# A grouped-query attention kernel whose start is rearranged: more filler matmuls, K of group 1 transposed later, exp of chunk 1 in two parts, one more share for VectorE

## Chip, cores, metric

One core of a Trainium2 chip. The time is what the device takes for one execution, in microseconds (us). Before: 522.71 us, median of 3 runs (522.05 to 522.73). Times inside a trace are us from the start of the span.

## The reference

```python
B, Hq, Hkv, Sq, Sk, D = 16, 32, 8, 288, 512, 128        # bf16
k = jnp.repeat(k, Hq // Hkv, axis=1); v = jnp.repeat(v, Hq // Hkv, axis=1)
scores = jnp.einsum("bhqd,bhkd->bhqk", q, k) * D ** -0.5
p = softmax(scores, axis=-1)
return jnp.einsum("bhqk,bhkd->bhqd", p, v)
```

There are 128 groups (batch and KV head), each with 1152 query rows against 512 keys.

## The kernel before

A group's transposed scores are cut into three chunks of 1536 columns; there are NS = 384 chunks. For chunk n, TensorE makes the scores S(n) (three matmuls of 512 columns, or two of 512 and four of 128), ScalarE takes the exp, and two chunks later TensorE multiplies by V (the PV batch, twelve matmuls of 129 columns, the last column giving the row sums). VectorE divides. In every sixth chunk VectorE computes the exp of the last 120 columns itself (a polynomial): the "share"; TensorE makes those scores in a small matmul of its own.

K of groups 0 and 1 is transposed on TensorE (`op_kt`, four 128x128 transposes into PSUM) and copied to SBUF by VectorE (`op_kc`); later groups come transposed from the DMA. The parts that matter:

```python
FIRST = 2; FIRST_SHARED = 6; LAG = 2; EVERY = 6; W = 120; WARM = 5
...
def shared(n):
    return FIRST_SHARED <= n < NS - NC and (n - FIRST_SHARED) % EVERY == 0
...
# op_exp: chunks 0, 1 and the last are taken in three parts of 512 columns
if n < FIRST or n == NS - 1:
    parts = [(x, x + BANK) for x in range(0, CH, BANK)]
...
@block.tensor
def _(eng):
    op_warm(WARM, BANK, ps_o[:, 1])          # 5 matmuls of ones, 512 columns
    op_warm(1, P, ps_o[:, 1])
    op_kt(0, range(1), 0)                    # K of group 0
    op_kt(0, range(1, NJ), 1)
    op_warm(1, P, ps_s[:, 1])                # one more, 128 columns
    for n in range(NS):
        op_s(n)
        if shared(n):
            op_sy(n)
        if n == 2:
            op_kt(1, range(NJ), 1)           # K of group 1; chunk 3 is its first user
        if n >= LAG:
            op_pv(n - LAG)
...
@block.scalar
def _(eng):
    op_kd(eng, 0)                            # load of K of group 0
    eng.activation(dum[:], ...)
    for (s, n) in need(eng, [("s_k0", 2)]):  # both copies of K of group 0 are made
        eng.wait_ge(s, n)
    op_kd(eng, 1)                            # load of K of group 1
    for n in range(NS):
        op_exp(n)
```

The first queries come by a transposing DMA on another queue.

## Time and profile before

| | before |
|---|---|
| span of the profiled run | 520.0 us |
| first score matmul, first exp | 4.41, 5.05 |
| six chunks in the middle | 7.98 |
| last exp starts, last VectorE instruction (the flag, the kernel's own check of its sums) starts | 515.82, 518.40 |

How to read it: the middle repeats every six chunks, so a change in the 7.98 counts 63 times and a change at either end once. The page's "chain that ended last" is followed back from the last instruction, at each step to what released it; it and the first microseconds are shown in the prediction. View: DMA issues of the kernel before, in the window 4.25 to 4.5 (what is loaded, KB, us from issue to landing):

```profile
kd_sb<-in_k_dram ACTq DMA_DIRECT2D x1, 128.0 KB, 3.0
```

K of group 1 was issued at 4.27 and landed at 7.26.

### The profile page before, as it was taken

The page shows a single profiled execution, that of the slowest core. Times are in us where ns is not written, and L with a number is a line of the kernel's source. Part 1 is how long each engine was busy: PE and PEld are TensorE (multiplying, and loading weights), DVE is VectorE, ACT ScalarE, POOL GpSimd, SP SyncE. Part 2 cuts the span into 40 slices and gives each one's busy share as a digit, 9 for nine tenths or more (in the row PEclk, how much of TensorE's full clock was granted, in tenths as well). Part 3 has the DMA queues.
Part 4 walks back from the last instruction along what each step waited for, and adds up shares of the span by engine and source line. Part 5 has one row for each costly group of instructions (what it writes and reads, how often), then busy time and mean ns, then how long its engine had stood idle before and what let it go on. Part 6 is the DMA issues. An engine that isn't in the chain of part 4 may idle for free.

```text
span 520.0 us, 15243 instructions
## 1 busy us (share of the span) xinstructions
PE 510.3 (98%) x6118; PEld 394.6 (76%) x6224; DVE 369.6 (71%) x1315; ACT 513.3 (99%) x393; POOL 79.8 (15%) x135
## 2 busy tenths in 40 slices
PE   8999999999999999999999999999999999999997
PEld 5777777777777777777777777777777777777776
DVE  2767767777777677676776776767767767677776
ACT  7999999999999999999999999999999999999997
POOL 2111111111111111111111111111111111111110
PEclk9999999999999999999999999999999999999999
DMA  9999999999999998999999989999998989998212
GB/s 186 237 218 230 267 194 248 225 213 210 219 233 256 208 245 201 235 248 240 215 241 209 209 225 220 241 185 209 229 240 232 227 194 201 192 234 198 86 69 93
DMA packets 253078, 110.06 MB, mean 212 GB/s; under 512 B 219728, under 2 KB 236752, under 8 KB 253008
## 3 DMA queue, kind: packets, MB, share of 16 engines
q1 hardware_dynamic: 252720, 108.82, 97.7%
q8 instruction: 49, 0.80, 0.7%
q10 hardware_dynamic: 288, 0.26, 0.2%
q14 instruction: 21, 0.17, 0.2%
HBM read 17.04 MB, written 37.75 MB: 105 GB/s over the span
## 4 chain that ended last, share of the span: by engine, by line
ACT 98%; DMA 1%; issue 1%; DVE 0%; PE 0%
ACT pt_sb L516 97%; DMA qt_sb<-in_q_dram 1%; ACT pt_sb L511 1%; PE ps_s L439 0%; DVE o_sb L585 0%; DVE o_sb L595 0%; PE ps_s L479 0%; DVE rl_sb L575 0%; PE ps_o L669 0%; DVE bad_sb L621 0%; DVE flag_i L734 0%; DVE bad_sb L618 0%
## 5 line engine op out<-in xcount | busy, mean ns | idle before, releaser
L516 ACT ACTIVATE pt_sb<-ps_s 128x1536 bf16<-128x1536 f32 (+2 forms) x384 | 508.8, 1441 | 0.0
L479 PE MATMUL ps_o<-v_sb,pt_sb 128*128 128x129 bf16 x4584 | 322.3, 220 | 1.1
L479 PEld LDWEIGHTS ps_o<-v_sb,pt_sb 128*128 128x128 bf16 x4584 | 282.8, 98 | 49.7 <-DVE o_sb L585 14.1
L439 PE MATMUL ps_s<-qt_sb,kt_sb 128*128 128x512 bf16 (+2 forms) x1430 | 290.4, 320 | 5.0 <-DMA qt_sb<-in_q_dram 0.5
L585 DVE TENSOR_TENSOR o_sb<-ps_o,rl_sb 128x384 bf16<-128x384 f32 x382 | 211.9, 555 | 9.3 <-DVE rl_sb L575 0.5
L439 PEld LDWEIGHTS ps_s<-qt_sb,kt_sb 128*128 128x128 bf16 x1536 | 123.9, 98 | 62.3 <-issue 1.1
L575 DVE RECIPROCAL rl_sb<-ps_o 128x3 f32<-128x3 f32 x382 | 68.1, 178 | 125.5 <-PE ps_o L479 124.0
L568 POOL COPY v_sb<-vd_sb 128x512 bf16<-128x512 bf16 x128 | 78.8, 616 | 429.1 <-PE ps_o L479 408.9
L549 DVE SCALAR_TENSOR_TENSOR u_sb<-u_sb,m_sb 128x120 f32<-128x120 f32 x126 | 35.6, 283 | 2.2
L556 DVE SCALAR_TENSOR_TENSOR pt_sb<-u_sb,e_sb 128x120 bf16<-128x120 f32 x63 | 17.8, 283 | 2.2
L549 DVE SCALAR_TENSOR_TENSOR u_sb<-m_sb 128x120 f32<-128x120 f32 x63 | 17.4, 277 | 0.0
L527 DVE TENSOR_SCALAR y_sb<-ps_o 128x120 f32<-128x120 f32 x63 | 15.9, 253 | 0.0
L540 DVE TENSOR_SCALAR m_sb<-t_sb 128x120 int32<-128x120 int32 x63 | 14.1, 223 | 2.2
L540 DVE TENSOR_SCALAR e_sb<-t_sb 128x120 int32<-128x120 int32 x63 | 13.6, 216 | 0.0
L450 PE MATMUL ps_o<-qt_sb,kt_sb 128*128 128x120 bf16 x63 | 13.6, 216 | 0.0
L533 DVE TENSOR_SCALAR t_sb<-y_sb 128x120 int32<-128x120 f32 x63 | 13.4, 213 | 0.0
L450 PEld LDWEIGHTS ps_o<-qt_sb,kt_sb 128*128 128x128 bf16 x63 | 6.2, 98 | 7.4
L511 ACT ACTIVATE pt_sb<-ps_s 128x512 bf16<-128x512 f32 x6 | 3.3, 616 | 2.3 <-PE ps_s L439 2.3
L411 DVE COPY kt_sb<-ps_o 128x128 bf16<-128x128 bf16 (+2 forms) x3 | 1.0, 336 | 6.2 <-PE ps_o L404 6.1
L613 DVE TENSOR_REDUCE st_sb<-rl_sb 128x1 f32<-128x72 f32 (+1 forms) x16 | 3.5, 216 | 0.0
L611 DVE TENSOR_REDUCE st_sb<-rl_sb 128x1 f32<-128x72 f32 (+1 forms) x16 | 3.5, 216 | 0.0
L417 PE MATMUL ps_o<-const-bfloat16-1.0 128*128 128x512 bf16 (+1 forms) x6 | 2.4, 570 | 0.9 <-PEq L752 0.9
(32 smaller groups left out, 12.0 us busy)
## 6 DMA issues: line engine op xcount, KB each, us to landing
out_dram<-o_sb SPq DMA_DIRECT2D x127, 288.0 KB, 3.7
vd_sb<-in_v_dram SPq DMA_DIRECT2D x31, 512.0 KB, 5.5
qt_sb<-in_q_dram SPq DMA_TRANSPOSE x128, 4.9
kt_sb<-in_k_dram SPq DMA_TRANSPOSE x32, 5.1
vd_sb<-in_v_dram SPq DMA_DIRECT2D x1, 384.0 KB, 4.6
out_dram<-o_sb SPq DMA_DIRECT2D x3, 96.0 KB, 1.6
kd_sb<-in_k_dram ACTq DMA_DIRECT2D x2, 128.0 KB, 2.7
vd_sb<-in_v_dram SPq DMA_DIRECT2D x1, 128.0 KB, 3.3
```

The source lines that it names most:

```text
L439: ins = emit(eng, w_x, lambda: eng.matmul(ps_s[:, n % 2, c:c + w], kt_sb[:, sl, j, gi, :], qg[:, t * P:t * P + w], start=True, stop=True))
L450: emit(eng, [("s_ev", n - LAG - 1)], lambda: eng.matmul(ps_o[:, (n - LAG) % 2, BANK - W:BANK], kt_sb[:, (g // UG) % NSLOT, j, g % UG, :], ...
L479: ins = emit(eng, w_x, lambda: eng.matmul(outs(r)[:, t - r % NC * TPC, :], pt(g, t, j), v_sb[:, sl, gi * NJ + j, 0:DV], start=(x == 0), st ...
L516: emit(eng, waits, lambda: eng.activation(d, s, ACTF.Exp, scale=scale)).then_inc(sem["s_e"], 1)
L527: emit(eng, [("s_yb", nth(n) - NB), ("s_pv", n - LAG + 1)], lambda: eng.tensor_scalar(out=y_sb[:, b], in0=ps_o[:, (n - LAG) % 2, BANK - W: ...
L533: emit(eng, [("s_ym", 2 * (nth(n) - NB)), ("s_y", nth(n))], lambda: eng.tensor_scalar(out=t_sb[:, b], in0=y_sb[:, b], scalar1=Y_MUL, scala ...
L540: emit(eng, [("s_yp", nth(n) - NB), ("s_yb", nth(n))], lambda: eng.tensor_scalar(out=dst[:, b], in0=t_sb[:, b], scalar1=mask, scalar2=bits ...
L549: lambda: eng.scalar_tensor_tensor(out=u_sb[:, b, x], in0=src, scalar=QUARTIC[x], in1=m, op0=ALU.add, op1=ALU.mult)
L556: lambda: eng.scalar_tensor_tensor(out=pt_sb[:, n % NPT, CH - W:CH], in0=u_sb[:, b, 2], scalar=QUARTIC[3], in1=e_sb[:, b].bitcast(FP32), o ...
L568: emit(eng, waits, lambda: eng.tensor_copy(v_sb[:, sl, gi * NJ:(gi + 1) * NJ, 0:D], vd_sb[:, sl, gi].rearrange("p (j d) -> p j d", d=D))). ...
L575: emit(eng, [("s_pv", r + 1)], lambda: eng.reciprocal(rl_sb[:, TPC * r:TPC * (r + 1)].unsqueeze(2), outs(r)[:, :, D:DV])).then_inc(sem["s_ ...
L585: emit(eng, waits, lambda: eng.tensor_tensor(out=o_sb[:, g % NO, t0:t0 + TPC, :], in0=outs(r)[:, :, 0:D], in1=rl_sb[:, TPC * r:TPC * (r + ...
```

## The change

Its intent: keep TensorE busy with matmuls of ones (the fillers) until the first queries land, so that its clock is fast sooner; put the first PV batch into the time in which TensorE waits for K of group 1; save one instruction of ScalarE in chunk 1; give VectorE a share in chunk 381 too, the first chunk of the last group.

```diff
-    FIRST_SHARED = 6
+    PARTS = {0: (1, 2, 3), 1: (2, 3), NG * NC - 1: (1, 2, 3)}
 ...
+    SHARED = list(range(2 * NC, NS - NC, EVERY)) + [NS - NC]
 ...
-            if n < FIRST or n == NS - 1:
-                parts = [(x, x + BANK) for x in range(0, CH, BANK)]
+            if n in PARTS:
+                parts = [(x * BANK, y * BANK) for (x, y) in zip((0,) + PARTS[n], PARTS[n])]
 ...
-            return FIRST_SHARED <= n < NS - NC and (n - FIRST_SHARED) % EVERY == 0
+            return n in SHARED
 ...
-            op_warm(1, P, ps_s[:, 1])
+            op_warm(6, P, ps_s[:, 1])
             for n in range(NS):
                 op_s(n)
                 if shared(n):
                     op_sy(n)
+                if n >= LAG:
+                    op_pv(n - LAG)
                 if n == 2:
                     op_kt(1, range(NJ), 1)
-                if n >= LAG:
-                    op_pv(n - LAG)
```

Cut: the bookkeeping of semaphore counts that follows from parts of unequal size, and the numbering of the shares.

More of the change, by code (lines that the diff above doesn't have):

```diff
@@ L372, in used, with part, ahead @@
             return max(b for b in range(NC) for t in range(b * TPC, (b + 1) * TPC) for j in range(NJ) if place(t, j)[0] == i)
+        def part(n, x):
+            return sum(x >= e for e in PARTS.get(n, (TPC,)))
+        def ahead(n):
+            return sum(len(PARTS[m]) - 1 for m in range(n))
         def ready(n, x):
-            if n < FIRST and x < TPC - 1:
-                return ("s_eb", n * (TPC - 1) + x + 1)
-            return ("s_e", n + 1 + (x if n == NS - 1 else 0))
+            p = part(n, x)
+            if n < FIRST and p < len(PARTS[n]) - 1:
+                return ("s_eb", ahead(n) + p + 1)
+            return ("s_e", n + 1 + (p if n == NS - 1 else 0))
         def sequence(b):
@@ L440, in op_s @@
                     ps_s[:, n % 2, c:c + w], kt_sb[:, sl, j, gi, :], qg[:, t * P:t * P + w], start=True, stop=True))
-                if n < FIRST and (c + w) % BANK == 0 and c + w < CH:
+                if n < FIRST and (c + w) % BANK == 0 and (c + w) // BANK in PARTS[n][:-1]:
                     ins.then_inc(sem["s_s0"], 1)
@@ L507, in op_exp @@
                 parts = [(0, CH - W)]
-            if n < FIRST or n == NS - 1:
-                parts = [(x, x + BANK) for x in range(0, CH, BANK)]
+            if n in PARTS:
+                parts = [(x * BANK, y * BANK) for (x, y) in zip((0,) + PARTS[n], PARTS[n])]
             for x, (c, e) in enumerate(parts[:-1]):
-                ins = emit(eng, [("s_s0", (TPC - 1) * n + x + 1)] if n < FIRST else waits, lambda: eng.activation(
+                ins = emit(eng, [("s_s0", ahead(n) + x + 1)] if n < FIRST else waits, lambda: eng.activation(
                     d[:, c:e], s[:, c:e], ACTF.Exp, scale=scale))
@@ L519, in shared @@
         def shared(n):
-            return FIRST_SHARED <= n < NS - NC and (n - FIRST_SHARED) % EVERY == 0
+            return n in SHARED
         def nth(n):
-            return (n - FIRST_SHARED) // EVERY + 1
+            return SHARED.index(n) + 1
         def op_y(n):
```

## The prediction

> **What bounds the kernel now.** I read the busy shares first. They are of little use alone, since two engines are full:
>
> ```profile
> PE 510.3 (98%) x6118; PEld 394.6 (76%) x6224; DVE 369.6 (71%) x1315; ACT 513.3 (99%) x393; POOL 79.8 (15%) x135
> ACT 98%; DMA 1%; issue 1%; DVE 0%; PE 0%
> ```
>
> The second line is the page's chain that ended last: nearly all of it is ScalarE's exp. The chain in order of time says where ScalarE's row begins and how it goes on (start, us, what):
>
> ```profile
> 0.82 3.54 DMA qt_sb<-in_q_dram
> 4.41 0.62 PE ps_s L439
> 5.05 1.09 ACT pt_sb L511 x2
> 7.60 5.61 ACT pt_sb L516 x5
> ...
> 21.23 0.05 issue
> 21.28 7.93 ACT pt_sb L516 x6
> ...
> 508.21 6.66 ACT pt_sb L516 x5
> 518.40 0.17 DVE flag_i L734
> ```
>
> The first queries land at 4.36, the first matmul starts at 4.41, the first exp at 5.05, and from there exp never stops until the tail at 516. The repeated group is six chunks in 7.93 + 0.05 = 7.98 us. So the change can only act in three places: before exp starts, in the first few chunks, or in the last ones. The whole middle (63 groups) is untouched.
>
> For the beginning I took the timeline of ScalarE and TensorE in windows so narrow that each instruction stands alone:
>
> ```profile
> 5.05 0.60 ACT L511 ACTIVATE pt_sb<-ps_s 128x512 bf16<-128x512 f32 x1 [2.33 <-PE ps_s L439]
> 6.50 0.62 ACT L511 ACTIVATE pt_sb<-ps_s 128x512 bf16<-128x512 f32 x1
> 6.97 0.63 ACT L511 ACTIVATE pt_sb<-ps_s 128x512 bf16<-128x512 f32 x1
> 7.93 1.51 ACT L516 ACTIVATE pt_sb<-ps_s 128x1536 bf16<-128x1536 f32 x1
> 9.26 1.52 ACT L516 ACTIVATE pt_sb<-ps_s 128x1536 bf16<-128x1536 f32 x1
> ```
>
> ```profile
> 5.66 0.57 PE L439 MATMUL ps_s<-qt_sb,kt_sb 128*128 128x512 bf16 x1
> 6.07 0.38 PE L439 MATMUL ps_s<-qt_sb,kt_sb 128*128 128x512 bf16 x1
> 6.29 0.38 PE L439 MATMUL ps_s<-qt_sb,kt_sb 128*128 128x512 bf16 x1
> 7.31 0.23 PE L404 MATMUL ps_o<-ident,kd_sb 128*128 128x128 bf16 x1
> 8.31 0.38 PE L439 MATMUL ps_s<-qt_sb,kt_sb 128*128 128x512 bf16 x1
> ```
>
> The 6.50, 6.97 and 7.93 lines are exp of chunk 1 in parts and of chunk 2: a part of 512 columns takes 0.475 us from start to start, a chunk of 1536 takes 1.33. In the second fence TensorE turns fast at about 6.05: score matmuls come 0.42 us apart before it and 0.215 after. The 7.31 line is the first transpose of K of group 1; the 8.31 line is the first score matmul of chunk 3, the first one that needs that K.
>
> **What the Trainium skill says.** "TensorE: Matmul & The Clock Gate", Part 1: The HAM clock gate, says TensorE starts at 1.2 GHz and goes to 2.4 GHz after a busy window of about 3.4 us, and that this window runs free of the kernel. The trace agrees on the two rates (0.42 against 0.215 us for 512 columns) and on the size of the delay (first matmul 0.86, fast at 6.05). Part 4 of the same page says transposes do not count as activity in the same way; no view here shows that. "ScalarE: Activation LUTs", What ACT_TABLE_LOAD costs, gives 186 ns plus 0.833 ns a column, of which neighbours overlap some 93 ns. The slope holds: 512 x 0.833 = 427 ns, so 50 ns of each 475 ns step is fixed, less than the 93 ns that the page's two figures leave. The trace's 50 ns is used.
>
> **The change part by part.**
>
> Six small matmuls of ones in place of one, 128 columns each. On a cold TensorE the transposes before them start 0.107 us apart (3.23, 3.52 for the first and the fourth), so five more add 0.53 us: the stream that ended near 3.74 now ends at 4.27, before the queries at 4.36. They delay nothing. What they can buy is an earlier fast clock. The window that ended at 6.05 began, by the skill's 3.4 us, at 2.64 and held the idle stretch from 3.74 to 4.41; it released the clock all the same. So filling that stretch should not be what decides; if the window is free-running, the phase does. Best case, fast by 4.41: the first score matmul takes 0.38 instead of 0.61, and the first exp starts 0.23 earlier. But exp of chunk 3 then waits for K of group 1, whose load lands at 7.27 (issued 4.27, 3.0 us to landing), so nearly all of the 0.23 is lost again there (below).
>
> Exp of chunk 1 in two parts instead of three. It saves one fixed 50 ns, so exp of chunk 2 starts at 7.88 instead of 7.93, if exp of chunk 3 can follow. It also makes the first part 1024 columns long: it ends at 6.50 + 0.853 + 0.19 = 7.54 (0.19 is 0.62 less 0.427), where the 512-column part ended at 7.12. Three of the twelve matmuls of the first PV batch read bank 0 of that chunk, so they now wait for 7.54.
>
> K of group 1 behind the first PV batch. Before: transposes at 7.31 to 7.49, VectorE's copy 7.74 to 8.16, first matmul of chunk 3 at 8.31, which is 0.82 after the last transpose. The PV batch (12 x 0.056 = 0.68 us) ran inside those 0.82 us and cost nothing. After: chunk 2's scores end at 7.16, nine PV matmuls run to 7.67, the three late ones to 7.84, transposes start at 7.84, the last at 8.02, and the first matmul of chunk 3 at 8.02 + 0.82 = 8.84, not 8.31. TensorE stands idle during the copy. What it wins is only the wait for the load, 7.16 to 7.31. Exp of chunk 3 can start at 8.84 + 2 x 0.215 + 0.38 + 0.03 = 9.68, against 9.26: 0.42 us later. Is there slack later to take it up? Before, chunk 3's scores were ready at 8.31 + 0.84 = 9.15, only 0.11 ahead of their exp, and that slack is already used in this sum. From there ScalarE runs chunk after chunk with nothing in between, so 0.42 stays. With the fast clock from 4.41 on: scores of chunk 2 end near 6.65, exp of chunk 1's first part runs 6.25 to 7.29, late PV matmuls 7.35 to 7.52, last transpose 7.70, chunk 3 at 8.52, its exp at 9.36, so +0.10. These two bound it: +0.10 to +0.42, middle +0.26.
>
> VectorE's share in chunk 381. Its exp has 120 columns fewer, 120 x 0.833 = 0.10 us. But a shared chunk in the middle gains less: the six-chunk group takes 7.98, where six full ones take 6 x 1.333 = 8.00, because exp of the chunk after waits for its scores (the 0.05 of issue at 21.23 and in every group). At the end: exp of 382 could start at 512.20 + 1.233 = 513.43, but its scores start at 512.66 and are there at 512.66 + 0.84 = 513.50; now it starts at 513.53. Gain 0.03. VectorE's eight added operations take some 2.0 us (213 to 283 ns each in the page's groups); they delay the evictions of batch 380 and 381, but in the group of chunk 378 the same work is caught up within two batches. Batch 382's reciprocal at 516.47 should stay where it is.
>
> Sum: +0.26 - 0.03 = +0.23 us, 522.71 to 522.94.
>
> **The rivals.** First, the filler wins more than I grant: fast clock always by 4.4, and transposes that are ready earlier. Against it: the K load lands at 7.27 whatever TensorE does, and chunk 3 follows a full 1.0 us after the first transpose. Even the old order with a fast clock from the start gains only 0.1. This rival makes 522.6. Second, the idle stretch mattered in the timed runs (their spread of 0.7 us, 522.05 to 522.73, is as large as what a late clock could cost): then the filler removes bad runs, and the median falls to about 522.3. Third, the clock turns fast later, say at 6.8: then chunk 1's two-bank part waits for its second bank too, exp of chunk 1 starts 0.2 later, and the loss is 0.6 to 0.7: 523.4. Fourth, the tail: VectorE is late for the last evictions, up to 0.3 us more.
>
> **Range and chances.** All terms together lie between -0.4 and +0.7 us; the runs before scatter by 0.7. So 522.9, with 522.1 to 523.6 for 8 in 10. Two per cent is 10.5 us; nothing here is a tenth of that: same 0.98, the rest split.
>
> **What would show it.** Right: exp of chunk 3 starts 0.1 to 0.4 later than 9.26; TensorE has a gap of about 0.6 us between the transposes of group 1 and chunk 3; groups of six still take 7.98; exp of chunk 382 moves up by no more than 0.1 within the tail. Wrong: the first exp at 4.82 and chunk 3's exp before 9.26 (filler wins), chunk 3's scores right behind the transposes, or the middle group no longer 7.98. A fast clock at another time than 6.05 would say that the phase, not the filler, moved the start; only several runs could tell these apart.

## The result

After: 522.15 us, median of 5 runs (522.0 to 522.44); before in the same rounds 522.27. Ratio 0.9998, 95% interval 0.9983 to 1.0013. (A ratio here is the mean time of one kernel's fast runs over the mean of the other's of the same rounds, so not quite the ratio of the medians.) The interval is 0.8 us wide to either side: the timed runs say "the same" and cannot tell +0.23 from 0. What happened must be read from traces. Here too care is needed: the execution whose trace the prediction was worked from took 521.67 us, less than any of the five timed runs before (521.84 to 522.73); the profiled one after took 522.00.

View: the page of the changed kernel, busy time and the chain that ended last.

```profile
PE 516.2 (99%) x6230; PEld 395.1 (76%) x6230; DVE 370.4 (71%) x1323; ACT 513.4 (99%) x392; POOL 79.8 (15%) x135
PE 98%; DVE 1%; DMA 0%; issue 0%
```

The chain has changed sides: 98% ScalarE before, 98% TensorE now. Yet the span differs by 0.3 us (520.3 against 520.0) and six chunks take 7.98 us in both. When a chain flips and nothing else does, the two engines were level, and the name in the chain was no proof of the bound. The experiments return to this.

View: single instructions of ScalarE, TensorE and VectorE in the changed kernel (start, us, engine, line, tiles, shape).

```profile
6.60 1.04 ACT L521 ACTIVATE pt_sb<-ps_s 128x1024 bf16<-128x1024 f32 x1
7.98 1.49 ACT L526 ACTIVATE pt_sb<-ps_s 128x1536 bf16<-128x1536 f32 x1
9.72 1.45 ACT L526 ACTIVATE pt_sb<-ps_s 128x1536 bf16<-128x1536 f32 x1 [0.25 <-PE ps_s L449]
```

```profile
5.33 0.54 PE L449 MATMUL ps_s<-qt_sb,kt_sb 128*128 128x512 bf16 x1
5.71 0.38 PE L449 MATMUL ps_s<-qt_sb,kt_sb 128*128 128x512 bf16 x1
7.70 0.23 PE L489 MATMUL ps_o<-v_sb,pt_sb 128*128 128x129 bf16 x1
7.88 0.22 PE L414 MATMUL ps_o<-ident,kd_sb 128*128 128x128 bf16 x1
8.30 0.42 DVE L421 COPY kt_sb<-ps_o 128x512 bf16<-128x512 bf16 x1 [3.97 <-PE ps_o L414]
8.88 0.38 PE L449 MATMUL ps_s<-qt_sb,kt_sb 128*128 128x512 bf16 x1 [0.61 <-DVE kt_sb L421]
```

The predicted sequence is there. The exp of chunk 2 follows that of chunk 1 after 1.38 us (1.43 before: one fixed 50 ns saved). The last three PV matmuls start at 7.70, held up by the two-part exp. Then come the transposes (7.88), the copy (8.30), and TensorE idles 0.61 us for it (last line). Exp of chunk 3 starts at 9.72, not 9.26, and waits for it. The flag comes at 518.84, 0.44 later than in the trace before.

It is tempting to stop here and charge the 0.44 us to the new order. One more view forbids it: DMA issues of the changed kernel, window 4.3 to 4.5.

```profile
kd_sb<-in_k_dram ACTq DMA_DIRECT2D x1, 128.0 KB, 3.5
```

Issued at 4.37, landed at 7.82. In this execution K of group 1 came 0.56 us later than in the trace before, and the transposes could not have started before 7.87 in any order; they started at 7.88. In this trace the new order cost 0.01 us. The loss is the later load (the transposes start 0.57 later, at 7.88 for 7.31), less what exp of chunk 2 had held up before anyway (0.13). The experiments must separate order, clock and load.

### The profile page after: what moved, and what is told of

It is laid out like the page before. It is cut to its first block, busy times and chain, and to the rows that moved or that the text cites. A ratio compares the mean times of both kernels' runs of the same rounds, so it can differ in the third digit from the quotient of the medians.

```text
span 520.3 us, 15370 instructions
## 1 busy us (share of the span) xinstructions
PE 516.2 (99%) x6230; PEld 395.1 (76%) x6230; DVE 370.4 (71%) x1323; ACT 513.4 (99%) x392; POOL 79.8 (15%) x135
## 4 chain that ended last, share of the span: by engine, by line
PE 98%; DVE 1%; DMA 0%; issue 0%
PE ps_o L489 50%; PE ps_s L449 47%; PE ps_o L460 1%; DMA kd_sb<-in_k_dram 0%; DVE o_sb L595 0%; PE ps_o L414 0%; DVE u_sb L559 0%; DVE rl_sb L585 0%; PE ps_s L427 0%; DVE kt_sb L421 0%; DVE o_sb L605 0%; DVE pt_sb L566 0%; PE ps_o L679 0%; DVE m_sb L550 0%; DVE t_sb L543 0%
## 5 line engine op out<-in xcount | busy, mean ns | idle before, releaser
L449 PE MATMUL ps_s<-qt_sb,kt_sb 128*128 128x512 bf16 (+2 forms) x1536 | 309.3, 324 | 0.6 <-DVE kt_sb L421 0.6
L521 ACT ACTIVATE pt_sb<-ps_s 128x512 bf16<-128x512 f32 (+1 forms) x5 | 3.2, 684 | 2.4 <-PE ps_s L449 2.4
```

Source lines behind the costliest of these rows:

```text
L449: ins = emit(eng, w_x, lambda: eng.matmul(ps_s[:, n % 2, c:c + w], kt_sb[:, sl, j, gi, :], qg[:, t * P:t * P + w], start=True, stop=True))
```

## The experiments

All twelve kernels gave correct results. For each trace I read five times. ("Front" and "behind" say where the transposes of K of group 1 stand against the first PV batch.) "Clock fast" is when TensorE's step between matmuls falls from 0.427 to 0.215 us (512 columns) or from 0.107 to 0.056 (128); it is worked out from the one step that is mixed (after: 5.33 to 5.71 is 0.38 us = 0.33 slow + 0.05 fast, so 5.66). In a1_kt_front the step changes earlier, among the fillers: they start 0.107 us apart up to 3.80, then 0.073, 0.058 and 0.060 (merged in narrow windows, one, two, three and four of them from 3.58 on last 0.31, 0.39, 0.45 and 0.51). "K landed" is the load of K of group 1. Then the first transpose of it, the first score matmul of chunk 3, and the flag.

| run | fillers | order | clock fast | K landed | transposes | chunk 3 | flag | flag less chunk 3 |
|---|---|---|---|---|---|---|---|---|
| before | 1 | front | 6.05 | 7.26 | 7.31 | 8.31 | 518.40 | 510.09 |
| after | 6 | behind | 5.66 | 7.82 | 7.88 | 8.88 | 518.84 | 509.96 |
| a1_kt_front | 6 | front | 3.83 | 7.44 | 7.49 | 8.49 | 518.47 | 509.97 |
| a2_one_filler | 1 | behind | 6.53 | 7.36 | 8.02 | 9.02 | 518.99 | 509.97 |
| a3_no381 | 6 | behind | 6.21 | 7.21 | 7.88 | 8.88 | 518.84 | 509.96 |
| b1_kt_behind | 1 | behind | 6.88 | 7.52 | 8.22 | 9.22 | 519.18 | 509.96 |
| b2_six_fillers | 6 | front | 5.80 | 7.76 | 7.81 | 8.82 | 518.78 | 509.96 |
| b3_shift_share | 1 | front | 5.36 | 7.48 | 7.53 | 8.53 | | |
| b4_every3 | 1 | front | 8.81 | 7.79 | 8.33 | 9.55 | | |
| b5_no_share | 1 | front | 9.17 | 7.62 | 8.36 | 9.65 | | |
| c1_kd1_early | 6 | front | 5.77 | 7.92 | 7.97 | 8.97 | 518.94 | 509.97 |
| c2_warm2 | 1 | front | 7.28 | 7.92 | 7.97 | 8.98 | 518.94 | 509.96 |
| c3_kd1_at_once | 6 | front | 8.86 | 4.93 | 8.98 | 9.97 | 519.94 | 509.96 |
| a4_chunk1_three | 6 | behind | 4.55 | 8.89 | 8.93 | 9.94 | 519.91 | 509.97 |

The last column (left out where the middle of the kernel was changed) is the key to everything: once chunk 3's scores have started, the end is fixed, at 509.97 us later within 0.01. Only the kernel before has 0.12 to 0.13 more: there chunk 3 was so early that TensorE had to wait for exp of chunk 2 next. The transposes and chunk 3 lie 0.99 to 1.01 us apart in all traces whose clock was fast by then. So in all of them but the kernel before, the start of the transposes decides the end.

The first four runs shared nine runs of the kernel before (median 521.70, mean 521.79).

**a1_kt_front.** Changed kernel, old order.

```diff
+                if n == 2:
+                    op_kt(1, range(NJ), 1)
                 if n >= LAG:
                     op_pv(n - LAG)
-                if n == 2:
-                    op_kt(1, range(NJ), 1)
```

> The changed kernel with the transposes of K of group 1 put back ahead of the first PV batch; everything else stays changed. Measured by the trace as (exp of chunk 3) minus (first score matmul), 4.85 us before and 5.22 after, and (last instruction of VectorE, the flag) minus (first score matmul), 513.99 before and 514.34 after, so that a later landing of the queries drops out. My theory (the copy of K lies bare behind the PV batch): 4.80 to 4.90 and 513.95 to 514.10, and TensorE has no gap over 0.1 us between transposes and chunk 3. Rival (the place of the transposes is indifferent, the start moved because of the clock or of the two-part exp): stays at 5.15 to 5.25 and 514.3. In the median either is under 0.4 us of 522, near the scatter.

Measured: exp of chunk 3 at 4.98 us after the first score matmul, the flag at 514.11, the first 0.08 above the expected range, the second 0.01; both are nearer to that range than to the rival's. Time 521.74 median, ratio 1.0 (0.9986 to 1.0014). View: TensorE, single instructions.

```profile
4.36 0.39 PE L449 MATMUL ps_s<-qt_sb,kt_sb 128*128 128x512 bf16 x1 [0.15 <-DMA qt_sb<-in_q_dram]
4.58 0.38 PE L449 MATMUL ps_s<-qt_sb,kt_sb 128*128 128x512 bf16 x1
7.49 0.23 PE L414 MATMUL ps_o<-ident,kd_sb 128*128 128x128 bf16 x1 [0.68 <-DMA kd_sb<-in_k_dram]
8.34 0.22 PE L489 MATMUL ps_o<-v_sb,pt_sb 128*128 128x129 bf16 x1
8.49 0.38 PE L449 MATMUL ps_s<-qt_sb,kt_sb 128*128 128x512 bf16 x1
```

Here the clock was fast before the first score matmul (0.22 us to the next), and the first exp came at 4.78. Nothing was gained: TensorE ran into the load of K and waited 0.68 us. The PV batch (to 8.34) again hid the copy. I had not reckoned that the load itself would move (7.44, not 7.26), which is the difference.

**a2_one_filler.** Changed kernel with one filler.

```diff
-            op_warm(6, P, ps_s[:, 1])
+            op_warm(1, P, ps_s[:, 1])
```

> The changed kernel with one matmul of ones instead of six. TensorE turned fast at 5.66 us after, at 6.05 before. My theory (a window that runs free of the kernel decides, the idle stretch of 0.5 us does not): fast at some time between 4.3 and 7.0, not tied to the filler; exp of chunk 3 at 5.2 us after the first score matmul, plus up to 0.1 if the clock turns late; time the same within 0.2 us. Rival (the filler brought the clock forward by 0.4 us): fast at 6.05 again or later, and chunk 3's exp 0.07 or more later than in the changed kernel.

Measured: fast at 6.53; chunk 3's exp 5.56 us after the first score matmul, 0.26 above the range of my theory; time 521.94, ratio 1.0002. The clock turned later than in any trace with six so far, which leans to the rival. The transposes came at 8.02 although K had landed at 7.36: the new order cost 0.61 us here.

**a3_no381.** Changed kernel without the new share.

```diff
-    SHARED = list(range(2 * NC, NS - NC, EVERY)) + [NS - NC]
+    SHARED = list(range(2 * NC, NS - NC, EVERY))
```

> The changed kernel without VectorE's share in chunk 381. From exp of chunk 380 to the first exp of chunk 383 it is 4.00 us before and 4.04 after. Theory A, formed from the trace after (TensorE is busy without a gap there and sets the pace; the share makes its small score matmul wait for VectorE's eviction): 4.00 again, the end 0.03 to 0.05 earlier. Theory B, as predicted (ScalarE sets the pace, the share shortens its row by 0.03): 4.07 or more, the end 0.03 or more later. Median: the same.

Measured: 4.00 us from exp of 380 to that of 383, as theory A says. The end, however, did not move as A expected: from exp of chunk 380 to the flag it is 7.53 us here and 7.54 in the changed kernel (7.54 or 7.55 in all traces with the share in 381, 7.53 or 7.54 in those without). The share in chunk 381 gains nothing; by these traces it costs 0.01 us. Time 521.90, ratio 1.0002. K had landed at 7.21, the transposes waited until 7.88: the new order held them back by 0.63.

**b1_kt_behind.** Kernel before with only the order changed.

```diff
+                if n >= LAG:
+                    op_pv(n - LAG)
                 if n == 2:
                     op_kt(1, range(NJ), 1)
-                if n >= LAG:
-                    op_pv(n - LAG)
```

> The kernel before with only the transposes of K of group 1 moved behind the first PV batch; chunk 1 still in three parts, one filler, no share in 381. My theory: exp of chunk 3 at 5.15 to 5.30 us after the first score matmul (4.85 before), the flag at 514.3 (513.99 before), a gap of TensorE of about 0.6 us before chunk 3. Rival (the loss needs the two-part exp of chunk 1, which holds up the late PV matmuls): 4.85 to 4.95 and 514.0 to 514.1. Time: +0.3 us, near the scatter.

Measured: exp of chunk 3 at 5.71 us and the flag at 514.83, worse than I expected; the rival, that the loss needs the two-part exp, is out. View: TensorE, single instructions.

```profile
7.54 0.22 PE L479 MATMUL ps_o<-v_sb,pt_sb 128*128 128x129 bf16 x1
8.22 0.22 PE L404 MATMUL ps_o<-ident,kd_sb 128*128 128x128 bf16 x1
9.22 0.38 PE L439 MATMUL ps_s<-qt_sb,kt_sb 128*128 128x512 bf16 x1 [0.61 <-DVE kt_sb L411]
```

K had landed at 7.52, so the old order would have had the transposes at 7.57; the PV batch stood before them from 7.54 to 8.22. The new order cost 0.65 us, more than predicted because the clock was late (6.88). Time: median 521.77, but the runs go from 521.62 to 522.37 (the profiled one was the 522.37), ratio 1.0001.

Next came four runs with nine runs of the kernel before (median 521.84, mean 522.01).

**b2_six_fillers.** Kernel before with six fillers.

```diff
-            op_warm(1, P, ps_s[:, 1])
+            op_warm(6, P, ps_s[:, 1])
```

> The kernel before with six matmuls of ones instead of one, nothing else. So far TensorE turned fast at 5.66, before 4.36 and at 6.21 us in the three traces with six, at 6.05, 6.53 and 6.88 in the three with one. My theory: the first score matmul of chunk 3 follows the last transpose of K of group 1 by 0.83 us whatever the clock, and these transposes wait for their load at 7.3 to 7.5; so the end is first score matmul of chunk 3 plus 509.97 to 510.1, and the time is the same as before within 0.15 us, even if the clock turns early. Rival (the filler is the gain of the change): clock fast before 6.0 and the time 0.2 us or more lower.

Measured: fast at 5.80, flag 509.96 after chunk 3, time 522.07 (mean 522.03), ratio 1.0001. An earlier clock, as the rival says, and no gain, as my theory says: K landed at 7.76.

**b3_shift_share.** Kernel before, shares one chunk later.

```diff
-    FIRST_SHARED = 6
+    FIRST_SHARED = 7
```

> The kernel before with VectorE's share moved one chunk on (7, 13, ... instead of 6, 12, ...), so that in the wait after a shared chunk no late PV matmuls stand ahead of the scores. Theory A (TensorE runs without a gap in the middle and sets the pace of 7.98 us for six chunks): 7.98 again, time the same within 0.3 us. Theory B (exp after a shared chunk waits for scores that stand behind four late PV matmuls, ScalarE sets the pace): 7.95 or less for six chunks, 1.9 us or more off the time.

Measured: 523.53, ratio 1.0031 (1.0017 to 1.0044), slower by about 1.5 us, which neither theory had. In the trace 7.98 or 7.99 holds in three of four groups, 8.09 or 8.10 in every fourth: 15 groups x 0.11 = 1.65 us. The lost step comes every 24 batches, where VectorE also makes its reductions over a batch entry; the trace shows how. In each of these 15 groups the first matmul of a PV batch waits 0.10 to 0.11 us and starts 0.06 after an eviction (VectorE's division) ends, and from the reductions to that eviction VectorE never pauses for more than 0.04. B is out: the groups without that step show no gain.

**b4_every3.** Kernel before, twice the shares.

```diff
-    EVERY = 6
+    EVERY = 3
```

> The kernel before with twice as many shares (every third chunk, 125 instead of 63). Theory A (TensorE sets the pace): six chunks take 7.98 to 8.00 us, the time does not fall by more than 0.2 us and may rise, as each share adds a small matmul; ScalarE shows longer waits. Theory B (ScalarE sets the pace, a share saves what it takes off the exp, 0.10 us less the wait after it): 7.96 or less, 1.3 us or more off the time.

Measured: 7.98 or 7.99 us for six chunks, time 523.07 median (522.13 to 523.21), ratio 1.0014. Twice the shares, nothing gained. Part of the loss is at the start. View: TensorE, single instructions.

```profile
7.05 0.63 PE L439 MATMUL ps_s<-qt_sb,kt_sb 128*128 128x512 bf16 x1
7.48 0.63 PE L439 MATMUL ps_s<-qt_sb,kt_sb 128*128 128x512 bf16 x1
8.33 0.31 PE L404 MATMUL ps_o<-ident,kd_sb 128*128 128x128 bf16 x1
8.76 0.24 PE L479 MATMUL ps_o<-v_sb,pt_sb 128*128 128x129 bf16 x1
9.55 0.38 PE L439 MATMUL ps_s<-qt_sb,kt_sb 128*128 128x512 bf16 x1
```

Score matmuls still lie 0.43 us apart at 7.48: the clock turned at 8.8. K was there at 7.79, but chunk 2's scores were not done before 8.33. This is what a late clock costs: 0.50 us in the start of the transposes, and chunk 3 follows their start after 1.22 us instead of 1.00. Against the 1.05 from K's landing to chunk 3 in the traces whose transposes waited only for K, chunk 3 is 0.71 us late here, and 0.98 in b5, whose clock turned at 9.17.

**b5_no_share.** Kernel before, no shares.

```diff
-            return FIRST_SHARED <= n < NS - NC and (n - FIRST_SHARED) % EVERY == 0
+            return False
```

> The kernel before without any share of VectorE. Theory A (TensorE needs 7.98 us for six chunks, ScalarE alone 6 x 1.333 = 8.00, a tie): 8.00 us for six, 1.2 us more in the time, TensorE waits now and then. Rival (a share is worth the 0.10 us by which it shortens an exp): 8.08 for six, 6.3 us more.

Measured: 527.73 us (four fast runs, 526.67 to 528.35), ratio 1.0104, 5.6 us more (means 527.62 and 522.01); 8.06 for six chunks. My figure was wrong and the rival's, 8.08 and 6.3, nearly right. View: TensorE in the middle of this run, merged, then the page's chain.

```profile
251.97 0.88 PE L479 MATMUL ps_o<-v_sb,pt_sb 128*128 128x129 bf16 x12
252.69 0.81 PE L439 MATMUL ps_s<-qt_sb,kt_sb 128*128 128x512 bf16 x3
253.34 0.84 PE L479 MATMUL ps_o<-v_sb,pt_sb 128*128 128x129 bf16 x12
```

```profile
ACT 97%; PE 1%; DMA 1%; DVE 0%; issue 0%
```

Every third PV batch now takes 0.72 us to the next scores (251.97 to 252.69), where 0.68 is the undisturbed step: TensorE waits for exp. These waits, 0.04 us in every third batch, are the whole difference between 7.98 and 8.06. In the changed kernel and in b4 there are none: from 20 to 500 us their matmuls keep the usual spacing (but for two in b4). So with one share in six, or two, TensorE sets the pace, at 7.98. That ScalarE alone sets the 8.06 is not shown: four of six exps here start 1.35 us after the one before, just when their last scores are there, where an exp in the kernel before that finds its scores ready follows after 1.33. Each engine waits for the other in turn. The shares' worth is 0.08 us, 63 times, or 5.0 of the 5.6 us; the rest I did not trace, but the clock turned late in this run too (9.17).

The last four shared eleven runs of the kernel before (median 522.15, mean 522.27).

**c1_kd1_early.** a1_kt_front, and the load of K of group 1 one wait earlier.

```diff
-            for (s, n) in need(eng, [("s_k0", 2)]):
+            for (s, n) in need(eng, [("s_k0", 1)]):
```

> The changed kernel with the transposes of K of group 1 back in front (as in a1_kt_front) and the load of that K issued one copy earlier (after the first copy of K of group 0, not the second: some 0.4 us). My theory (chunk 3's scores come 0.83 us after the last of these transposes, and the transposes wait for the load): load at 6.9 to 7.1 instead of 7.45, chunk 3's scores start at 7.8 to 8.2, then TensorE waits for exp of chunk 2 instead; the flag at 518.2 to 518.35 against 518.40 before, 0.1 to 0.2 us off the time. Rival (the earlier load takes bandwidth from the first queries or the next ones): first score matmul later than 4.55, no gain.

Measured: issued at 3.88, landed at 7.92, after 4.0 us, where most traces have 3.0 to 3.6. The profiled run won nothing. The timed runs are 521.41 to 522.23, median 521.69, ratio 0.9989 (0.9976 to 1.0002): the lowest ratio here, but the interval still holds 1, and the profiled run was one of its slow ones. That it beats the kernel before is not shown. The trace rather speaks against it: the packets of this load (DMA queue 10) began to move at 5.92, no earlier than in the kernel before (5.94), where it was issued 0.38 later.

**c3_kd1_at_once.** The same with that pacing wait taken out (the load has its own buffer and its own semaphore, so nothing races); it is issued at 1.29.

```diff
-            for (s, n) in need(eng, [("s_k0", 2)]):
-                eng.wait_ge(s, n)
             op_kd(eng, 1)
```

> The same with the load of K of group 1 issued straight after that of group 0, with no wait. My theory: it shares the engines with the first queries, which land 0.2 to 0.6 us later (4.36 so far), and everything moves by as much: time 0.1 to 0.5 us more than before. Rival (the queue has room then): queries as before, transposes of group 1 as soon as TensorE is free (6.7 to 7.2), flag at 518.2 to 518.35.

Measured: the first queries landed at 5.23 instead of 4.2 to 4.5, the first exp started at 5.92, the flag at 519.94. Time 523.34, ratio 1.0015 (six runs, 521.92 to 523.92). My theory held and was too small. TensorE idled 1.07 us before those queries despite six fillers, and its clock turned only at 8.86.

**c2_warm2.** Kernel before, fewer matmuls of ones at the very start.

```diff
-    WARM = 5
+    WARM = 2
```

> The kernel before with two instead of five matmuls of ones of 512 columns at the start, so that TensorE idles some 1.3 us more before the first transposes. Theory A (the idle stretches before the first queries make the clock turn late in some runs, which is what the change's filler prevents): most runs turn fast only after 7 us, the profile shows scores 0.43 us apart up to chunk 2, the median is 0.4 to 1.2 us above that of before, and the runs lie wide apart. Rival (the time at which the clock turns is chance and has nothing to do with the filler): fast at 4.3 to 7 as in most traces, median within 0.2 us of before.

Measured: fast at 7.28; median 522.68 (522.03 to 522.78), mean 0.22 above before's, ratio 1.0005 (0.9992 to 1.0018). It does not settle the question. The median is 0.53 above before's, as theory A has it, the mean much less; and b4 and b5, whose first six chunks are the same program as before's, with all five matmuls, turned later still (8.81, 9.17). In the trace K landed late too, at 7.92, and chunk 2's scores were done just before.

**a4_chunk1_three.** Changed kernel, exp of chunk 1 in three parts.

```diff
-    PARTS = {0: (1, 2, 3), 1: (2, 3), NG * NC - 1: (1, 2, 3)}
+    PARTS = {0: (1, 2, 3), 1: (1, 2, 3), NG * NC - 1: (1, 2, 3)}
```

> The changed kernel with exp of chunk 1 in three parts again. In the trace after, the three late PV matmuls waited from 7.52 to 7.70 for the two-part exp. My theory: this wait goes, the transposes follow the scores of chunk 2 by 0.69 to 0.72 us when the clock is fast by then (0.92 in the trace after), chunk 3's scores come 0.1 to 0.2 us earlier, exp of chunk 2 starts 0.05 later, which costs nothing; end 0.1 to 0.2 us earlier where the clock turns by 6 us, the same where it turns later. Rival (the two-part exp is a gain of 0.05 us): the end 0.05 later. In the median either is lost in the scatter.

Measured: the wait in the PV batch is gone (twelve matmuls from 6.78 to 7.46 without a gap), but the transposes did not follow. Views: TensorE, single instructions; then DMA issues in the window 3.6 to 4.7.

```profile
7.40 0.22 PE L489 MATMUL ps_o<-v_sb,pt_sb 128*128 128x129 bf16 x1
8.93 0.23 PE L414 MATMUL ps_o<-ident,kd_sb 128*128 128x128 bf16 x1 [1.31 <-DMA kd_sb<-in_k_dram]
9.94 0.38 PE L449 MATMUL ps_s<-qt_sb,kt_sb 128*128 128x512 bf16 x1 [0.61 <-DVE kt_sb L421]
```

```profile
kd_sb<-in_k_dram ACTq DMA_DIRECT2D x1, 128.0 KB, 4.6
```

The earliest clock but one (4.55), everything ready, and yet the second latest flag of the table (519.91): K came at 8.89. Time 522.35 (521.76 to 523.07), ratio 0.9997. So runs are late for two reasons, clock and load, and a late run alone does not tell which.

## Why the prediction was right, and where its steps were not

The time lay in the range and the class was right: 522.15 against 522.9 predicted. The median of before in the same rounds was 0.44 lower than the one I started from, so most of the distance is scatter; the predicted difference of +0.23 lies inside the interval of the ratio, and so does 0. A forecast of no change at all would have been right too: that the time came out right confirms none of the steps, and they are judged here by the traces.

**What bounds the kernel: half wrong.** I read ScalarE as the bound from the chain. Shares taken out made TensorE wait for exp (8.06), shares doubled gave no gain (7.98) and TensorE no pause: in the middle TensorE sets the pace. The conclusion drawn from it, that only start and end can change anything, survived, because 7.98 held before and after.

**The filler: "delays nothing" right, "should not be what decides" probably wrong.** With six fillers and queries in time the clock was fast at 3.83, 4.55, 5.66, 5.77, 5.80 and 6.21; with one, at 5.36, 6.05, 6.53, 6.88, 8.81 and 9.17. In 31 of the 36 pairs the six-filler run is earlier. c3, where the idle stretch came back through late queries, turned at 8.86, and c2, with more idle time earlier, at 7.28. It is twelve traces and a chance process, so I call it likely. But b2 shows that it buys no time in a typical run (mean 522.03 against 522.01): chunk 3 waits for K, not for the clock. What it can spare is a late clock as in b4 and b5, two of the six traces with one filler, where chunk 3 came 0.71 and 0.98 us late. Whether it removes bad runs, the second rival, stays open: b2's five runs lie within 0.27 us where the nine of before beside them spread over 1.02, but the six-filler runs of c1 and a4 spread over 0.82 and 1.31. The prediction also read its trace as agreeing with the 3.4 us that it cites; by its own two numbers the delay was 6.05 - 0.86 = 5.2.

**Exp of chunk 1 in two parts: right.** It moved exp of chunk 2 by 0.05 us (1.38 for 1.43), delayed the late PV matmuls (7.70 in the trace after), and won nothing there, since exp of chunk 3 waited for its scores. (a4 was to test it, and K's late landing hid the answer.)

**K behind the PV batch: mechanism right, size tied to the wrong constant.** The 0.83 us from the last transpose to chunk 3 is in every trace whose clock was fast by then, the idle TensorE of 0.61 in every trace with the new order. The term that failed is "load lands at 7.27": it is no constant. In the twelve traces that issued it in the old place it came between 7.21 and 8.89, median 7.57. The order holds back transposes whose K is there by 0.01 us (after), 0.61 (a2), 0.63 (a3), 0.65 (b1), 0 (a4), and of that the end feels a little less where exp of chunk 2 would have held up chunk 3 anyway. At the assumed landing the sum is good: in a3, with K at 7.21, exp of chunk 3 started at 9.72 and the flag came 0.44 later than in the trace before, where +0.42 and 9.68 were predicted for a clock at 6.05. So the mechanism holds, and that the cost is one figure does not. For the 0.44 between the two profiled runs before and after, it was the load that differed. The third rival, a later clock with a loss of 0.6 to 0.7, is close to what a2 and b1 show: clock at 6.53 and 6.88, flag 0.59 and 0.78 later.

**The share in chunk 381: wrong, harmless.** Predicted -0.03, measured +0.01. The mis-sized term is "six full ones take 8.00": without shares they take 8.06 in b5. So in the middle a share is worth 0.08 us, more than the 0.02 I took; at the end, where TensorE already sets the pace, it is worth nothing. VectorE did catch up before the last evictions, as predicted: counted from exp of chunk 380, batch 382's reciprocal starts at 5.61 (5.60 before).

So four parts, with worths in one run of about 0 to -1.0 (filler, where the clock would have been late), 0 (two-part exp), 0 to +0.65 (order), +0.01 (share): no gain is left over, and the load's own scatter of up to 1.7 us hides the rest. Open: what makes the load of K take 3.0 us in one run and 4.6 in another, and whether c1's earlier issue is a gain. The traces narrow the first: in all but c3 the load's packets begin at 5.5 to 6.2 us, and the last one ends between 6.73 (a3) and 8.51 (a4), so the spread lies in its last packets.

## What to carry to other kernels

Where two engines are level, the chain names one of them by a hair; take away or double the work that was moved between them before believing it. Work placed in front of a produce-copy-consume step must not be the work that hid the copy: put the producer first and let the batch fill its latency. And before charging a later start to a reordering, look at when the data landed in both traces.

## What the Trainium skill lacked or had wrong

- "TensorE: Matmul & The Clock Gate", Part 1: it gives the turn as about 4 us into sustained activity, give or take 0.5 us, and warns of run-to-run variation. Activity starts at 0.86 us here, with idle stretches in it; the turn lay between 3.83 and 9.17, thus 3.0 to 8.3 us in, and it tended to be earlier where the idle stretch before the queries was filled. The page has no word on how much idle time inside a window still lets the clock turn.
- "ScalarE: Activation LUTs", What ACT_TABLE_LOAD costs: 186 ns fixed, some 93 ns of it overlapped, leaves 93 ns for each instruction in a row. Here it is 50 ns (start to start 0.477 us for 512 columns, less 0.427), and merging two parts saved 0.05.
- "DMA: Bandwidth & Descriptors", Anatomy of one DMA: its fit for the GpSimd path, 2.0 us plus bytes over 436 GB/s, gives an estimate of 2.3 us for 128 KB. The load of K of group 0, on ScalarE's queue, took 2.1 to 2.5; the same load for group 1, with other transfers under way, 3.0 to 4.6. I found no figure there for that spread, which is larger than the change studied here.
- No page that I looked at has the time from a transpose into PSUM through VectorE's copy to the first matmul that uses it: 0.83 us for 128x512 here (from the start of the last transpose), in every trace whose clock was fast.
